# A three-stage attention and gated-layer kernel: partition maxima on TensorE, weight chunks two a unit, loads behind the first queries, shared score slots, a Prelu gate

## The chip, the cores and the metric

One program runs on one core of one Trainium2 chip. The metric is the device time of one execution in microseconds. The kernel before took 1237.77 us, the median of three runs (1237.25 to 1241.06). Matrix products are float32-accurate: every operand is held as a high and a low float16 half, and a product is three float16 matmuls.

## The reference

```
q_pool = q.reshape(B, H, S//2, 2, D).mean(axis=3)          # B 4, H 8, S 1152, D 64
scores = q_pool @ k^T / 8;  attn = exp(scores - max)
attn   = attn / (sum(attn) + 1e-9);  x = attn @ v           # x becomes 2304 x 512
h = x @ w_in                                                # 512 x 2048
g = h if h >= 1;  0 if h <= -1;  (h + 1)^2 / 4 between
y = g @ w_out                                               # 2048 x 512
out = max(y @ w1, y @ w2, y @ w3) @ w_out2                  # 512 x 768, 768 x 512
```

The weights arrive as 64-bit floats and are turned to float32 on the chip, chunk by chunk.

## The kernel before

The attention runs in 48 **units**, one for each batch, block of 192 pooled queries and pair of heads: 4 batches x 3 blocks x 4 pairs, so units 0 to 11 are the first batch. In a unit TensorE makes three score tiles of 128 x 1152 (`soft`, words `s0`, `s1`, `s2`); for each, VectorE takes the row maximum (L380), ScalarE turns it into a bias (L381) and takes the exponential with its row sum (L382). The exponentials are then turned (`turned`, words `t0`, `t1`, `t2`; `t-` is the third one of the unit before). In the first batch TensorE turns all three tiles in float32 (L418) and ScalarE copies them out (L429, L431); in later batches only the third goes this way, and two go through a float16 split and a transposing DMA. `shares` (word `r`) makes the reciprocals of the row sums, spreads them over 64 columns each (L396), lets TensorE turn them (L398, L399) and copies the result out (L401, L402). `av` (word `a1`) multiplies with the values of the unit before.

Score tiles and turned tiles come from one PSUM pool of two slots, handed out in the order of the code. The third turned tile's slot also holds the turned reciprocals.

Beside attention, word `d` takes one step of the two dense layers, from unit 5 on: `up_steps` makes two blocks of 128 rows of h for one block of tokens (L520) and gates them, `down_steps` makes one block of y (L545). The gate is one ScalarE pass (L525), three VectorE passes (L526 to L528), one ScalarE pass to float16 (L529) and one VectorE pass for the low half (L530).

Word `w` takes one step of preparing w_in and then w_out, in the first batch alone: load a chunk of 64-bit words, make float32 of it (`to_f32`: one ScalarE pass, L156, and four VectorE passes, L157 to L162), take its squares on ScalarE, and, with a scale per row, split it in halves (L148, L149). The table W_STEPS says how many `w` words of a unit act. The maxima over partitions that scale the whole weight are taken by GpSimd's partition_all_reduce (L214 for w_in, L244 for w_out). k and v of a batch come at the times in K0, V0 (first batch) and K1, V1: load, square, and split, where `split` puts the high half on GpSimd and the low half on VectorE (L259, L260).

What sets the order: TensorE's instructions stand in the order of the words (manual order). The other engines' streams and the issue order of the DMAs, all on SyncE's queue, come from the compiler's list scheduler, with priorities shifted by the code. Each engine runs its own stream in order. After the 48 units the rest of the dense steps run beside the loading of w1, w2, w3, and then the last stage, bound to TensorE.

Of the kernel before, what the change touches and what calls it, by code (L numbers as in the profile page):

```python
# [52 lines left out]
def body(ctx: ExitStack, tc: tile.TileContext, q, k, v, w_in, w_out, w1, w2, w3, w_o2, out):  # L53
    nc = tc.nc
# [207 lines left out]
    first = []  # L262

    def load(x, b, p, key):
        if b == 0 and key == "k" and p:

            if p == 1:
                first.append(ptp.tile([P, 2, 2 * KT, NB], F16, tag="pt", name="kn0"))
            w = 2 * KT * D
            n = first[0].rearrange("p a b c -> p (a b c)").bitcast(F32)[:, (p - 1) * w:p * w].rearrange(  # L270
                "p (a b c) -> p a b c", a=2, b=KT)
        else:
            n = nat.tile([P, 2, KT, D], F32, tag="nat", name=f"{key}n{b}_{p}")
# [596 lines left out]
```

## Time and profile before

| What | Value |
|---|---|
| median of three runs | 1237.77 us |
| the profiled execution | 1240.77 us |
| its span | 1239.0 us |
| TensorE busy | 1080.9 us (87%) |
| VectorE busy | 880.2 us (71%) |
| ScalarE busy | 744.0 us (60%) |
| GpSimd busy | 128.2 us (10%) |

The span runs from the first to the last instruction; the execution lasts 1.8 us longer. Busy shares are means over stages that differ: the first batch ends about 302 us into the span, the last unit about 867 us, and the last stage starts about 963 us.

### The profile page before, as it was taken

The numbers are of one execution on the slowest core, as the hardware profiler recorded it, in microseconds if no ns is written. First come the engines' busy times: TensorE is split into PE (matmuls) and PEld (weight loads), VectorE is DVE, ScalarE is ACT, GpSimd is POOL, SyncE is SP. The second block draws the span as 40 slices with busy tenths as digits, with TensorE's granted clock in tenths as the row PEclk, the third lists the DMA queues.
The fourth block names the chain that finished last, engine by engine and source line by source line (L and its number), as shares of the span: only waits on it lengthen the run. The fifth ranks groups of instructions, "written<-read, shape, count | busy, mean of one in ns | idle before, by whom it ended". The sixth has DMA issues, their size and how long they took to land. (4 is left out here: it accounts for less than half of the span.)

```text
span 1239.0 us, 26628 instructions
## 1 busy us (share of the span) xinstructions
PE 1080.9 (87%) x11058; PEld 885.8 (71%) x11058; DVE 880.2 (71%) x1550; ACT 744.0 (60%) x1337; POOL 128.2 (10%) x114
## 2 busy tenths in 40 slices
PE   2446577789999998999998999999887999999998
PEld 1234366577888887788887888888886776767774
DVE  4973586776999999989899999888798652322220
ACT  4865476776777787778788777778554411122111
POOL 1110000111100021210011300000221020100000
PEclk9668688799999998999999999999898999999999
DMA  7743135035865679865669866656544220000001
GB/s 227 229 133 94 69 98 153 14 81 143 165 110 110 122 138 185 176 127 112 114 116 190 169 110 102 110 99 121 182 131 133 75 67 17 10 27 18 17 18 43
DMA packets 273752, 134.89 MB, mean 109 GB/s; under 512 B 229088, under 2 KB 256736, under 8 KB 272608
## 3 DMA queue, kind: packets, MB, share of 16 engines
q1 hardware_dynamic: 273632, 133.20, 47.7%
q8 instruction: 86, 1.41, 0.5%
q14 instruction: 34, 0.28, 0.1%
HBM read 62.39 MB, written 9.44 MB: 58 GB/s over the span
## 5 line engine op out<-in xcount | busy, mean ns | idle before, releaser
L366 PE MATMUL sc<-kst,qst 128*64 128x512 f16 (+3 forms) x1152 | 176.2, 342 | 55.8 <-ACT pf L382 15.8
L769 PE MATMUL p<-yh,wm 128*128 128x288 f16 x1728 | 216.7, 287 | 6.5 <-POOL yh L740 5.4
L545 PE MATMUL py<-g,wou 128*128 128x192 f16 x2304 | 204.4, 250 | 14.9 <-ACT g L529 5.8
L545 PEld LDWEIGHTS <-wou 128*128 128x128 f16 x2304 | 194.1, 100 | 24.8 <-issue 21.8
L520 PE MATMUL ph<-xh,win 128*128 128x192 f16 x2304 | 204.8, 250 | 7.3 <-POOL xh L259 3.1
L380 DVE TENSOR_REDUCE st<-sc 128x1 f32<-128x1152 f32 x144 | 194.5, 1351 | 20.7 <-PE sc L366 20.3
L769 PEld LDWEIGHTS <-wm 128*128 128x128 f16 x1728 | 169.8, 98 | 53.0 <-issue 7.6
L520 PEld LDWEIGHTS <-win 128*128 128x128 f16 x2304 | 196.8, 100 | 10.2 <-issue 8.1
L382 ACT ACTIVATE pf<-sc,st,esc 128x1152 f32<-128x1152 f32 x144 | 188.7, 1310 | 4.2
L366 PEld LDWEIGHTS <-qst 128*64 128x64 f16 (+1 forms) x1152 | 85.2, 108 | 116.5 <-issue 54.0
L418 PE MATMUL tr<-ident,pf 128*128 128x128 f32 x648 | 97.8, 303 | 42.1 <-ACT pf L382 34.0
L418 PEld LDWEIGHTS tr<-ident,pf 128*128 128x128 f32 x648 | 82.3, 159 | 54.5 <-ACT pf L382 40.5
L436 DVE TENSOR_TENSOR hl<-pf,hl 128x1152 f16<-128x1152 f32 x72 | 98.3, 1366 | 4.8 <-ACT hl L435 2.1
L777 ACT ACTIVATE h<-mx 128x288 f16<-128x288 f32 x48 | 21.2, 442 | 132.1 <-DVE mx L775 132.1
L774 DVE TENSOR_TENSOR mx<-p,mx 128x288 f32<-128x288 f32 x48 | 21.9, 456 | 106.3 <-PE p L769 105.7
L454 PE MATMUL av<-pt,vhl 128*64 128x192 f16 x1944 | 87.6, 248 | 0.3 <-DMA pt<-hl 0.2
L454 PEld LDWEIGHTS <-vhl 128*64 128x64 f16 x1944 | 79.9, 110 | 9.9 <-issue 9.4
L435 ACT ACTIVATE hl<-pf 128x1152 f16<-128x1152 f32 x72 | 83.4, 1158 | 0.8
L529 ACT ACTIVATE g<-t,dgs 128x384 f16<-128x384 f32 x96 | 57.7, 608 | 40.5 <-DVE t L528 40.3
L381 ACT ACTIVATE st<-st,esc 128x1 f32<-128x1 f32 x144 | 41.4, 288 | 54.3 <-DVE st L380 54.1
L530 DVE SCALAR_TENSOR_TENSOR g<-t,dgs,g 128x384 f16<-128x384 f32 x96 | 62.8, 661 | 5.3 <-ACT g L529 5.2
L786 PE MATMUL po<-wo,h 128*128 128x512 f16 x288 | 64.3, 379 | 0.0
(169 smaller groups left out, 1323.4 us busy)
## 6 DMA issues: line engine op xcount, KB each, us to landing
kn<-in_k_dram SPq DMA_DIRECT2D x16, 576.0 KB, 4.3
vn<-in_v_dram SPq DMA_DIRECT2D x16, 576.0 KB, 4.3
raw_m<-in_moe_w_dram SPq DMA_DIRECT2D x12, 768.0 KB, 4.7
raw_in<-in_moe_w_in_dram SPq DMA_DIRECT2D x8, 1024.0 KB, 5.6
qn<-in_q_dram SPq DMA_DIRECT2D x24, 256.0 KB, 3.4
raw_ou<-in_moe_w_out_dram SPq DMA_DIRECT2D x10, 512.0 KB, 4.5
qst<-qst SPq DMA_DIRECT2D x48, 96.0 KB, 2.2
y_d<-ys SPq DMA_DIRECT2D x48, 96.0 KB, 2.0
```

Source lines behind the costliest of these rows:

```text
L366: nc.tensor.matmul(sc[m0:m1, n0:n1], qst[b, i, p][who][:, var, m0:m1], ks[:, h, n0:n1], start=(var == 0), stop=(var == 1))
L380: nc.vector.tensor_reduce(out=m, in_=sc, axis=AX.X, op=ALU.max, negate=True)
L382: nc.scalar.activation(out=pf, in_=sc, func=AF.Exp, bias=nb, scale=e, accum_out=sums[b, i, p][:, who:who + 1])
L418: nc.tensor.transpose(tr[:, c * P:(c + 1) * P], pf[:, c * P:(c + 1) * P], ident)
L435: nc.scalar.activation(out=hl[:, 0], in_=pf, func=AF.Copy)
L436: nc.vector.tensor_tensor(out=hl[:, 1], in0=pf, in1=hl[:, 0], op=ALU.subtract)
L454: nc.tensor.matmul(acc[64 * h:64 * h + 64], vhl[b, p][:, vi, h, c, :], pt[:, h, pi * KT + c, :], start=(c == 0 and e == 0), stop=(c == KT ...
L520: nc.tensor.matmul(ph[:, a], win[:, wi, kt, ff * P:(ff + 1) * P], x[:, xi, kt], start=(kt == 0 and e == 0), stop=(kt == KD - 1 and e == 2))
L530: nc.vector.scalar_tensor_tensor(out=g[:, 1, fs, :], in0=t2, scalar=gs, in1=g[:, 0, fs, :], op0=ALU.mult, op1=ALU.subtract)
L545: nc.tensor.matmul(py, wou[:, ff // 2, wi, ff % 2, m * P:(m + 1) * P], g[:, gi, ff, :], start=(ff == 0 and e == 0), stop=(ff == NF - 1 and ...
L769: nc.tensor.matmul(ph[:, :NB2], wm[:, wi, i, kt, ff * P:(ff + 1) * P], yh[:, yi, kt, n0:n0 + NB2], start=(kt == 0 and e == 0), stop=(kt == ...
L786: nc.tensor.matmul(po, h2t[b][:, hi, ff, t * P:(t + 1) * P], wo[:, wi, ff, :], start=(ff == 0 and e == 0), stop=(ff == NF2 - 1 and e == 2))
```

## The change

The list of edits:
- `all_max` is new: it turns a column, spread over 128, with TensorE, and VectorE takes the maximum along the free axis. It takes the place of both partition_all_reduce.
- In the first batch the words stand in another order (ORDER), and `t2` closes its own unit.
- W_AT names which `w` words of a unit act: two in units 0 to 3, four in unit 4, three in 5 to 7, two in 8; two more steps exist, since the maximum of w_in and the first loads of w_out are steps of their own. Three chunks of w_out are loaded ahead.
- k and v loads of the first batch have other times (K0, V0) and their own buffers; the second loads wait in the queue until the first queries' copies have been issued.
- The spreading copy of the reciprocals goes to GpSimd and covers two of the three columns.
- The gate is Prelu with slope 0.5 on ScalarE, then two VectorE passes instead of three; one factor 0.5 per batch falls away.

```diff
-K0 = ((-2, -2, -2), (-1, 0, 0), (0, 1, 1), (3, 5, 5))
+K0 = ((-2, -2, -2), (-1, 0, 1), (0, 2, 3), (3, 5, 6))
-W_STEPS = {0: 3, 1: 3, 2: 2, 3: 1, 4: 2, 5: 3, 6: 3, 7: 2, 8: 2}
+W_AT = {0: "13", 1: "13", 2: "13", 3: "13", 4: "0123", 5: "123", 6: "123", 7: "123", 8: "01"}
-ORDER = {True: "s0 t- d d r s1 t0 q s2 t1 a1 w d d w w",
-         False: "s0 t- d d r s1 t0 a1 s2 t1 q w d d w w"}
+ORDER = {True: "s0 w0 r d s1 d w1 t0 a1 q t1 w2 s2 d d w3 t2",
+         False: "s0 t- d d r s1 t0 a1 s2 t1 q d d"}
+    def all_max(dst, x, n, key):
+        ps = psg.tile([P, 512], F32, tag="g1", name=f"max_{key}")[:, :n * P].rearrange("p (a b) -> p a b", a=n)
+        for a in range(n):
+            nc.tensor.transpose(ps[:, a], x[:, a:a + 1].to_broadcast([P, P]), ident)
+        nc.vector.tensor_reduce(out=dst, in_=ps, axis=AX.X, op=ALU.max)
-        nc.gpsimd.partition_all_reduce(U_in, um[:, 0:2], P, RMAX)
+        yield
+        all_max(U_in, um, 2, "in")
-        nc.gpsimd.partition_all_reduce(U_ou, um[:, 1:2], P, RMAX)
+        all_max(U_ou, um[:, 1:2], 1, "ou")
+        for h in range(3):
+            fetch(h)
+        yield
-        rb = tp.tile([P, 3, 64], F32, tag="rb", bufs=2, name=f"rb{b}_{i}_{p}")
-        nc.vector.tensor_copy(out=rb, in_=sm.rearrange("p (a o) -> p a o", o=1).to_broadcast([P, 3, 64]))
+        rb = tp.tile([P, 2, 64], F32, tag="rb", bufs=2, name=f"rb{b}_{i}_{p}")
+        nc.gpsimd.tensor_copy(out=rb, in_=sm[:, 0:2].rearrange("p (a o) -> p a o", o=1).to_broadcast([P, 2, 64]))
-            nc.scalar.activation(out=t2, in_=ph, func=AF.Relu, scale=hh, bias=0.5)
-            nc.vector.tensor_scalar(out=rl, in0=t2, scalar1=1.0, scalar2=None, op0=ALU.min)
-            nc.vector.scalar_tensor_tensor(out=t2, in0=t2, scalar=2.0, in1=rl, op0=ALU.mult, op1=ALU.subtract)
-            nc.vector.tensor_tensor(out=t2, in0=t2, in1=rl, op=ALU.mult)
+            nc.scalar.activation(out=t2, in_=ph, func=AF.Prelu, scale=hh, bias=-1.0, alpha=0.5)
+            nc.vector.tensor_scalar(out=t2, in0=t2, scalar1=1.0, scalar2=0.0, op0=ALU.add, op1=ALU.max)
+            nc.vector.scalar_tensor_tensor(out=t2, in0=t2, scalar=1.0, in1=t2, op0=ALU.min, op1=ALU.mult)
-    first_k = issued["k"]
-    with tc.issue_after(first_k):
+    with tc.issue_after(issued["q"]):
```

What the code alone doesn't show is where the instructions then stand. On SyncE's queue, at the start of the program, before (kn, qn, vn are loads of k, q, v; raw_in is a chunk of w_in; kst and qst are turned k and q, and the two DMAs from qst to qst swap its halves):

```order
L297 DMA_TRANSPOSE kst_0_125<-kpre_0_124 128x18x128
L340 DMA_TRANSPOSE qst_0_0_149<-qpre_0_0_140 128x6x128
L274 DMA kn_159<-in_k_dram 128x2x576
L180 DMA raw_in_1_161<-in_moe_w_in_dram 128x2048
L342 DMA qst_0_0_149<-qst_0_0_149 64x768 x2
L304 DMA vn_0_178<-in_v_dram 128x2x576
```

And now:

```order
L302 DMA_TRANSPOSE kst_0_125<-kpre_0_124 128x18x128
L345 DMA_TRANSPOSE qst_0_0_149<-qpre_0_0_140 128x6x128
L347 DMA qst_0_0_149<-qst_0_0_149 64x768 x2
L279 DMA kn_1_159<-in_k_dram 128x2x576
L185 DMA raw_in_1_161<-in_moe_w_in_dram 128x2048
L309 DMA vn_0_178<-in_v_dram 128x2x576
```

The two swapping copies of the first queries moved ahead of a k load and of the second weight chunk.

On TensorE, in unit 2 (third pair of heads, first block), before (sc is a score tile, tr a turned tile, rb the spread reciprocals; of each score tile the first row stands):

```order
L366 MATMUL sc_0_2_1_526<-kst_2_214,qst_0_2_381 128x512
...
L418 MATMUL tr_0_2_0_547<-ident,pf_0_2_0_500 128x128 x9
...
L366 MATMUL sc_0_2_2_558<-kst_2_214,qst_0_2_381 64x512
...
L418 MATMUL tr_0_2_1_576<-ident,pf_0_2_1_534 128x128 x9
L449 MATMUL av_0_1_587<-pt_0_1_356,vn_1_313 64x192 x18
...
L366 MATMUL sc_0_3_0_630<-kst_3_404,qst_0_2_381 128x512
...
L418 MATMUL tr_0_2_2_645<-ident,pf_0_2_2_572 128x128 x9
```

And now:

```order
L371 MATMUL sc_0_2_1_504<-kst_2_259,qst_0_2_398 128x512
...
L423 MATMUL tr_0_2_0_528<-ident,pf_0_2_0_478 128x128 x9
L454 MATMUL av_0_1_539<-pt_0_1_350,vn_1_309 64x192 x18
L423 MATMUL tr_0_2_1_560<-ident,pf_0_2_1_512 128x128 x9
...
L371 MATMUL sc_0_2_2_571<-kst_2_259,qst_0_2_398 64x512
...
L423 MATMUL tr_0_2_2_612<-ident,pf_0_2_2_585 128x128 x9
...
L371 MATMUL sc_0_3_0_625<-kst_3_437,qst_0_2_398 128x512
...
L403 MATMUL tr_0_2_2_612<-ident,rb_0_2_641 128x128
```

Before, score tiles and turned tiles took turns, so every score tile got one slot and every turned tile the other. Now two score tiles follow each other, then two turned tiles, then one of each, and the slots change hands. The value product moved between the first two turned tiles, and the turned reciprocals stand right behind the next unit's first score tile.

On GpSimd, around the first partition maximum, before (qn and qpre are pooled queries and their halves, xh the halves of x, ISA an instruction around the custom one):

```order
L259 TENSOR_SCALAR qpre_1_2_1061<-qn_1_2_1057,sqq_1_2_1062 128x6x64
L335 TENSOR_TENSOR qn_2_0_1471<-qn_2_0_1471 128x6x64
L214 ISA
L214 ISA U_in<-um_in 128x2
L259 ISA
L259 TENSOR_SCALAR qpre_2_0_1475<-qn_2_0_1471,sqq_2_0_1476 128x6x64
L259 TENSOR_SCALAR xh_0_899<-xf_0_445,Uv_446 128x768
```

And now:

```order
L340 TENSOR_TENSOR qn_1_0_701<-qn_1_0_701 128x6x64
L274 TENSOR_SCALAR qpre_1_0_705<-qn_1_0_701,sqq_1_0_706 128x6x64
L401 COPY rb_0_1_498<-sm_0_1_299 128x128
L340 TENSOR_TENSOR qn_1_2_1081<-qn_1_2_1081 128x6x64
L274 TENSOR_SCALAR kpre_3_436<-kn_3_319,sb_121 128x18x64
L274 TENSOR_SCALAR qpre_1_2_1085<-qn_1_2_1081,sqq_1_2_1086 128x6x64
L401 COPY rb_0_2_641<-sm_0_2_477 128x128
```

The custom instruction with its two companions is gone from the stream, and copies of reciprocals stand between the query and key work.

## Rows read from the trace of the kernel before

**Rows 1.** Busy time by stretch: PE, PEld, DVE, ACT, POOL, granted clock, DMA share, GB/s.
```profile
24.53:115.54 91.01, 52.03 (x341) 35.86 (x342) 66.70 (x128) 64.08 (x101) 9.74 (x9) 0.74 0.52 147
115.54:150.22 34.68, 14.84 (x91) 10.12 (x90) 14.27 (x29) 13.40 (x22) 2.49 (x4) 0.61 0.29 98
150.22:302.00 151.78, 123.20 (x1124) 100.22 (x1123) 110.26 (x191) 108.03 (x183) 16.99 (x18) 0.91 0.36 101
302.00:432.00 130.00, 126.69 (x1573) 111.48 (x1573) 117.60 (x200) 101.64 (x191) 13.29 (x13) 0.99 0.66 124
432.00:552.00 120.00, 108.60 (x1307) 95.17 (x1303) 109.41 (x195) 91.24 (x170) 22.46 (x18) 0.96 0.80 158
642.00:732.00 90.00, 79.39 (x956) 69.55 (x953) 84.77 (x154) 68.33 (x127) 16.78 (x14) 0.96 0.84 161
732.00:867.00 135.00, 134.70 (x1714) 119.43 (x1713) 119.95 (x185) 107.69 (x201) 3.45 (x4) 1.00 0.59 106
867.00:963.00 96.00, 78.77 (x834) 72.65 (x833) 82.38 (x144) 52.16 (x85) 19.37 (x7) 0.89 0.48 150
963.00:1239.00 276.00, 270.90 (x2000) 192.23 (x1999) 84.88 (x184) 58.69 (x121) 11.69 (x12) 1.00 0.10 31
```

**Rows 2.** Timeline, GpSimd, unit 4: start, duration, instruction [idle before <- releaser].
```profile
117.89 0.99 POOL L335 TENSOR_TENSOR qn<-qn 128x384 f32<-128x384 f32 x1 [24.49 <-DMA qn<-in_q_dram]
126.97 0.37 POOL L214 PARTITION_ALL_REDUCE U_in<-um_in  x1 [8.09 <-issue]
134.33 0.58 POOL L259 TENSOR_SCALAR qpre<-qn,sqq 128x384 f16<-128x384 f32 x1 [6.99 <-issue]
```

**Rows 3.** Timeline, VectorE, the same stretch.
```profile
127.38 0.21 DVE L472 TENSOR_SCALAR Uv<-U_in,Uv 128x1 f32<-128x1 f32 x1 [7.27 <-POOL U_in L214]
...
134.94 0.62 DVE L260 SCALAR_TENSOR_TENSOR qpre<-qn,sqq,qpre 128x384 f16<-128x384 f32 x1 [6.85 <-POOL qpre L259]
```

**Rows 4.** Groups of instructions: busy us, mean ns of one | idle before.
```profile
L211 DVE TENSOR_REDUCE um_in<-sum_in 128x1 f32<-128x512 f32 x1 | 0.7, 692 | 0.2 <-PE sum_in L209 0.2
L396 DVE COPY rb<-sm 128x192 f32<-128x192 f32 x48 | 16.9, 352 | 1.4
L259 POOL TENSOR_SCALAR qpre<-qn,sqq 128x384 f16<-128x384 f32 x24 | 18.8, 783 | 143.9 <-ACT py L549 83.3 <-ACT st L381 20.6 <-ACT pt L424 12.4
L280 ACT ACT_TABLE_LOAD x1 | 1.3, 1283 | 0.7 <-PEq L857 0.7
```

**Rows 5.** Timeline, GpSimd, behind the second partition maximum.
```profile
235.93 0.90 POOL L259 TENSOR_SCALAR xh<-xf,Uv 128x768 f16<-128x768 f32 x1 [7.15 <-DVE st L380]
```

**Rows 6.** Timeline, TensorE, the first score tile.
```profile
16.09 1.14 PE L366 MATMUL sc<-kst,qst 128*128 128x512 f16 x3 [9.47 <-DMA qst<-qpre]
23.37 1.12 PE L366 MATMUL sc<-kst,qst 128*128 128x512 f16 x3 [6.14 <-DMA qst<-qst]
```

**Rows 7.** DMA issues: KB each, median us to landing.
```profile
qst<-qst SPq DMA_DIRECT2D x48, 96.0 KB, 2.2
```

**Rows 8.** Waits, 24.53 to 302 us: us in total, times, longest.
```profile
POOL qn L335 <- DMA qn<-in_q_dram: 114.1, 9, 29.4
DVE st L380 <- PE sc L366: 19.9, 14, 4.5
```

**Rows 9.** Gate multiplication L528 by stretch: DVE busy (count), clock, DMA share, GB/s.
```profile
150.22:302.00 151.78, 8.34 (x14) 0.91 0.36 101
432.00:552.00 120.00, 8.40 (x14) 0.96 0.80 158
642.00:732.00 90.00, 6.30 (x11) 0.96 0.84 161
867.00:963.00 96.00, 5.37 (x10) 0.89 0.48 150
```

**Rows 10.** Timeline, VectorE and GpSimd together, in unit 11.
```profile
285.92 1.38 POOL L335 TENSOR_TENSOR qn<-qn 128x384 f32<-128x384 f32 x1 [1.79 <-DVE rl L526]
...
286.48 1.23 DVE L528 TENSOR_TENSOR t<-t,rl 128x384 f32<-128x384 f32 x1
```

More of the change, by code (lines that the diff above doesn't have):

```diff
@@ L4 @@
 import concourse.tile as tile
-from concourse import bass_isa, mybir
+from concourse import mybir
 from concourse._compat import with_exitstack
@@ L16 @@
 DRAM = bass.MemoryType.DRAM
-RMAX = bass_isa.ReduceOp.max
-RADD = bass_isa.ReduceOp.add
 HO = (1, 0)
 POOL_FIRST = 10
-K0 = ((-2, -2, -2), (-1, 0, 0), (0, 1, 1), (3, 5, 5))
-V0 = ((0, 0, 0), (3, 4, 4), (6, 7, 7), (9, 10, 10))
+K0 = ((-2, -2, -2), (-1, 0, 1), (0, 2, 3), (3, 5, 6))
+V0 = ((0, 2, 3), (3, 5, 6), (5, 7, 8), (8, 10, 11))
 K1 = (-2, 0, 2)
 V1 = (1, 2, 3)
-W_STEPS = {0: 3, 1: 3, 2: 2, 3: 1, 4: 2, 5: 3, 6: 3, 7: 2, 8: 2}
+W_AT = {0: "13", 1: "13", 2: "13", 3: "13", 4: "0123", 5: "123", 6: "123", 7: "123", 8: "01"}
 OW = 130
 OD0, T0 = -150, 48
-ORDER = {True: "s0 t- d d r s1 t0 q s2 t1 a1 w d d w w",
-         False: "s0 t- d d r s1 t0 a1 s2 t1 q w d d w w"}
+ORDER = {True: "s0 w0 r d s1 d w1 t0 a1 q t1 w2 s2 d d w3 t2",
+         False: "s0 t- d d r s1 t0 a1 s2 t1 q d d"}
 DEPTH = 1
@@ L226, in w_ou_steps, with fetch @@
         sts.append(one[:, 4:6].rearrange("p a b -> p (a b)").bitcast(F32))
-        for h in range(NG):
+        raws = {}
+        def fetch(h):
             at_ = {0: 6, 1: 4, 3: 6}.get(h)
@@ L237, in w_ou_steps @@
                 load_q.dma_start(out=raw[:, f], in_=words(w_out[ff * P:(ff + 1) * P, :]))
-            to_f32(sts[h], raw.rearrange("p a b c -> p (a b) c"))
+            raws[h] = raw
+        for h in range(3):
+            fetch(h)
+        yield
+        for h in range(NG):
+            to_f32(sts[h], raws.pop(h).rearrange("p a b c -> p (a b) c"))
             nc.scalar.activation(out=wou[:, 0, 0].bitcast(BF16), in_=sts[h].rearrange("p (a b) -> p a b", a=2),
                                  func=AF.Square, accum_out=mx[:, h:h + 1])
+            for x in {0: (3,), 2: (4,), 4: (5,), 5: (6,), 6: (7,)}.get(h, ()):
+                fetch(x)
             yield
@@ L260, in split @@
         nc.vector.scalar_tensor_tensor(out=lo, in0=x, scalar=s, in1=hi, op0=ALU.mult, op1=ALU.subtract)
-    first = []
     def load(x, b, p, key):
[L265 to L273, printed above, removed]
+        n = nat.tile([P, 2, KT, D], F32, tag="nat", name=f"{key}n{b}_{p}")
         load_q.dma_start(out=n, in_=x[b, 2 * p:2 * p + 2].rearrange("h (p c) d -> p h c d", p=P))
@@ L393, in shares @@
         nc.vector.tensor_scalar(out=sm, in0=sm, scalar1=1e-9 * 2.0 ** 12, scalar2=None, op0=ALU.add)
-        rb = tp.tile([P, 3, 64], F32, tag="rb", bufs=2, name=f"rb{b}_{i}_{p}")
         nc.vector.reciprocal(out=sm, in_=sm)
-        nc.vector.tensor_copy(out=rb, in_=sm.rearrange("p (a o) -> p a o", o=1).to_broadcast([P, 3, 64]))
+        rb = tp.tile([P, 2, 64], F32, tag="rb", bufs=2, name=f"rb{b}_{i}_{p}")
+        nc.gpsimd.tensor_copy(out=rb, in_=sm[:, 0:2].rearrange("p (a o) -> p a o", o=1).to_broadcast([P, 2, 64]))
         r, half = R[b, i, p], slice(64, P)
-        nc.tensor.transpose(rs[:, 0:P], rb[:, 0:2].rearrange("p a o -> p (a o)"), ident)
-        nc.tensor.transpose(rs[:, P:2 * P], rb[:, 2, 0:1].to_broadcast([P, P]), ident)
+        nc.tensor.transpose(rs[:, 0:P], rb.rearrange("p a o -> p (a o)"), ident)
+        nc.tensor.transpose(rs[:, P:2 * P], sm[:, 2:3].to_broadcast([P, P]), ident)
         nc.scalar.activation(out=r, in_=rs[:, :NB], func=AF.Copy)
@@ L485, in scales @@
         hu = small.tile([P, 1], F32, tag="hu", name=f"hu{b}")
-        hh = small.tile([P, 1], F32, tag="hh", name=f"hh{b}")
         nc.vector.tensor_scalar(out=hu, in0=U_in[:, 1:2], scalar1=Uv[b][:, NPAIR:NPAIR + 1],
                                 scalar2=None, op0=ALU.mult)
-        nc.vector.tensor_scalar(out=hh, in0=Uv[b][:, NPAIR + 1:NPAIR + 2], scalar1=0.5, scalar2=None, op0=ALU.mult)
         gd = small.tile([P, 1], F32, tag="dgd", name=f"dgd{b}")
@@ L495, in scales @@
         nc.vector.reciprocal(out=gs, in_=gd)
-        dst[b] = hh, gd, gs
+        dst[b] = Uv[b][:, NPAIR + 1:NPAIR + 2], gd, gs
     room = dict(h=(psg, "g1"), y=(psg, "g1"), t2=tp, n=2)
@@ L608, in body @@
     behind, todo = {}, []
-    words_left = [3] * len(units)
     def attend(n, word):
@@ L637, in attend @@
         elif kind == "w":
-            words_left[n] -= 1
-            if words_left[n] < W_STEPS.get(n, 0):
+            if num in W_AT.get(n, ""):
                 with shift(OW):
```

1 line of the change is left out of this document (removed).

## The prediction

> **What bounds the kernel now.** I read the busy time by stretch first, cut where the stages change [rows 1]. Three kinds of stretch are to be seen. From 732 to 867 us TensorE is busy 134.7 of 135.0 us, and in the last stage, from 963 us, 270.9 of 276.0: there only TensorE's own work counts. From 302 to 432 us it is nearly so, 126.7 of 130.0. In the two stretches where the next batch's k and v are prepared (432 to 552, 642 to 732) TensorE lacks 11.4 and 10.6 us, and VectorE is busy 91% and 94%: VectorE bounds. The first batch, before 302 us, is bound by no engine: VectorE is busy 66.7 of 91.0 us in units 0 to 3, 14.3 of 34.7 in unit 4, 110.3 of 151.8 in units 5 to 11, and TensorE's granted clock is 0.74, 0.61 and 0.91. So the second thing to read is what the first batch waits for, from the timeline of unit 4 and the waits of the first batch.
>
> **Partition maxima by TensorE.** In unit 4 the custom reduction runs only 0.37 us, but GpSimd stands 8.09 us ahead of it and 6.99 us behind it for nothing that the trace shows [rows 2]. VectorE waits in both gaps, 7.27 us for the maximum and 6.85 us for the query half that GpSimd makes next [rows 3]: 14.1 us. In its place come two turns on TensorE and one VectorE maximum of 128 x 256; the nearest row, 128 x 512, takes 0.69 us [rows 4], so between nothing and 0.7, and with the two hops between engines I take 1.5 us for all. The gain is 12.6 us; at least 6 (only one gap goes, the other being covered by what else is late), at most 14.1. The second reduction, for w_out, leaves the same kind of gap, 7.15 us, in front of the half of x that TensorE needs [rows 5]. Most of it lies beside other work; I take 3, bounds 0 and 7.2.
>
> **Loads behind the first queries.** The first score tile's second half starts at 23.37 us, having waited 6.14 us for the swapped halves [rows 6]; such a copy lands in 2.2 us [rows 7], but behind it in the queue stood a k load and a 1 MB chunk. With the copies ahead, the tile can be ready some 4 us earlier. The k load and the chunk come later in exchange, and so does what they feed. I take 2 us gained; bounds 4 gained, 3 lost.
>
> **Two slots for scores and turns, weight steps spread.** A score tile no longer waits for the exponential of the tile ahead of it, only for the tile two places back. VectorE waited 19.9 us in 14 pieces for scores between 24.5 and 302 us [rows 8]; that is what the sharing can shorten, and it leaves VectorE free to take the weight steps, which were three a unit early and are now two. For units 0 to 3 VectorE's 66.7 us at the 94% that it reaches in 642 to 732 [rows 1] would need 71 us instead of 91: at most 20 gained, at least nothing, since the same conversions stand in one stream with the maxima. I take VectorE at 80%, 83 us: 8 gained. For units 5 to 11 VectorE loses 8.3 us of gate products [rows 9] and seven copies of 0.352 [rows 4], which leaves 99.5 us; TensorE's 123.2 us bound the stretch instead, 127 us at the 97% of the stretch behind it. So at most 25 gained, at least 0. I take 10 beyond the 3 above, nearer to zero, because scores, maximum, exponential and turn still follow each other within a unit. The turned reciprocals now stand right behind the next first score tile; if their copy is late, TensorE waits there with the second score tile behind it. TensorE's clock should rise with its share in these units; I count nothing for it.
>
> **Prelu gate and the GpSimd copy.** The product L528 goes, 96 times. Prelu takes the place of a Relu of the same size from the same slot, and the two passes left have the forms of L526 and L527, so I price them as before; the trace has no Prelu, and a slower one by 0.1 us would lie on ScalarE, which is idle a quarter of the time. VectorE gets back 8.40 and 6.30 us of products in the two k and v stretches [rows 9], and with half as many copies, 12 or 13 of 0.352 us [rows 4], 4.4 us more: 19.1 us, where TensorE lacks 22.0 in all. I take two thirds, 13 us, since some of the lack is waiting on loads and on ScalarE; bounds 0 and 22. From 302 to 432 TensorE has 3.3 us to give; I take 1. Between 867 and 963 ten gates give back 5.4 us [rows 9] of VectorE's 82.4 in 96 us [rows 1]; loads and weight work fill the rest, so 2, bounds 0 and 5.4. From 732 to 867 and from 963 on, nothing.
>
> The copy costs GpSimd a third of the 0.783 us that 128 x 384 takes [rows 4], 0.26 us, or all of it at most. What hides it is the turn of the third tile and the next score tile ahead of the reciprocals.
>
> The trace shows GpSimd and VectorE hindering each other: the gate product that started 0.56 us after a query sum on GpSimd took 1.23 us [rows 10], twice what the others take (8.40 us for 14). The Trainium skill, page "SBUF — State Buffer", section "Who interferes with whom", says why: the two share one port pair, which one of them holds for a whole instruction. By that rule each of the 48 copies can hold up a VectorE pass by its own 0.26 us, and the copy moved gives back 0.09 us instead of 0.352; in the k and v stretches that is 3 us less, and the sum below would be 49 instead of 52. I leave the sum as it is, since a copy need not meet such a pass.
>
> **The sum.** First batch 12.6 + 3 + 2 + 8 + 10 = 35.6; then 1 + 13 + 2: together 51.6 us. The profiled execution took 1240.77 us (its span 1239.0 and 1.8 around it), so 1189.2 by its own time; the median of the three runs lies 3.0 us lower, which would be 1186. I predict 1188 us.
>
> **The rivals.**
> - *Only the stalls go.* The conversions, the maxima and the exponentials of the first batch stand in line as before, and sharing slots only moves the wait. For it: in units 0 to 3 the same chunks pass through the same VectorE stream, and the loads come in at 147 GB/s all the while [rows 1]. Against it: VectorE's waits for scores. Gains 12.6 + 3 + 2 + 10 + 2 = 30: 1211 us. Chance 0.17.
> - *The first batch fills up.* Units 0 to 3 take 71 us and units 5 to 11 take 127; with 19 in the k and v stretches and 4 in the tail the gain is 12.6 + 2 + 20 + 25 + 1 + 19 + 4 = 84: 1157 us. For it: VectorE does reach 91 to 94% elsewhere. Chance 0.10.
> - *Slower: the copy on GpSimd becomes the wait.* GpSimd works in order, and it stands 114.1 us in nine waits for query loads, 12.7 each [rows 8]. A copy of reciprocals queued behind such a wait holds TensorE at the turned reciprocals, and the second score tile with it. In the new stream the copies of units 0 to 3 do stand behind query work. Four full holds, 51 us, use up the sum; from there it decides. With five, 63 us, the time is 1240.8 - 51.6 + 63 = 1252. Against it: those waits began when GpSimd had nothing else to do, so little of them falls after the sums are known. Chance 0.05.
> - *Prelu needs another table than the exponential.* Then ScalarE would load tables twice a gate at 1.283 us [rows 4], 96 times: 246 us on an engine that has half that free, so well over 1300 us. Against it: the new program holds one table load, as the old one did. Chance 0.01.
> - *Nothing to measure*, gains and holds cancel: 1240 us, chance 0.03.
>
> On the fourth, the Trainium skill, page "ScalarE: Activation LUTs", section "Table sets: the hidden batching unit", gives about 2.7 us for each change of set and names the cheap functions in every set without naming Prelu. By that figure the price would be some 500 us; no run shown here has a Prelu.
>
> **How the numbers follow.** The forecast has 0.64; its own range is 1172 to 1205 us (terms at half and at one and a half of the uncertain 36 us, rounded). The range for 8 in 10 takes in the first rival with its spread and most of the way to the second: 1160 to 1222. Left out are the lower half of the second rival, the slower cases and the unchanged one. A difference under 0.3%, about 3.7 us, can't be told from none. Faster: 0.64 + 0.17 + 0.10 = 0.91; same 0.03; slower 0.05 + 0.01 = 0.06.
>
> **What would show it.** Right: no gaps of 7 to 8 us on GpSimd around unit 4, and unit 4 at some 20 us instead of 34.7; the first score tile's second half before 20 us; the first batch's end near 266 us instead of 302; TensorE's lack in the k and v stretches at 9 instead of 22 us; 96 VectorE passes fewer, and 48 copies on GpSimd of about 0.26 us. Wrong: if the first batch ends later than 285 us (then the first rival), if TensorE waits long for a GpSimd copy at the turned reciprocals (the third), or if table loads stand between the gates (the fourth). What would make the forecast wrong without any of these is a weight load or the w_out halves coming late in the new order, with TensorE waiting at the first block of y.

## The result, and the profile after

The changed kernel takes 1203.7 us (median of four runs, 1202.4 to 1207.5) where the kernel before took 1239.4 beside it: a ratio of 0.971, interval 0.967 to 0.975. The forecast was 1188 with an own range of 1172 to 1205. The direction is right and the time lies inside both ranges, in its own range by 1.3 us; the gain is 36 us instead of 51.6, and the time is nearer to the first rival's 1211 than to 1188. The profiled span is 1201.7 us against 1239.0.

The busy time by stretch, cut near the same places of the program as [rows 1]; columns: stretch, length, then busy us (and instructions) of PE, PEld, DVE, ACT, POOL, granted clock, DMA share, GB/s.
```profile
20.10:109.34 89.24, 53.88 (x336) 37.95 (x338) 68.45 (x128) 67.65 (x104) 10.06 (x13) 0.77 0.66 198
109.34:131.48 22.14, 14.68 (x107) 9.91 (x102) 17.76 (x35) 13.59 (x21) 3.79 (x4) 0.80 0.31 103
131.48:274.11 142.63, 119.61 (x1117) 98.75 (x1118) 92.51 (x163) 106.94 (x182) 20.10 (x24) 0.91 0.34 93
404.00:523.00 119.00, 108.22 (x1351) 94.82 (x1347) 104.80 (x176) 91.17 (x172) 23.07 (x25) 0.99 0.82 162
612.00:700.00 88.00, 80.10 (x982) 70.69 (x981) 78.91 (x139) 68.88 (x129) 17.58 (x18) 0.98 0.83 167
700.00:832.00 132.00, 131.47 (x1674) 116.30 (x1672) 105.69 (x151) 104.08 (x197) 5.93 (x14) 1.00 0.60 109
```
The first batch ends at 274 us; 266 was expected. Unit 4 (second row) lost 12.5 us. Units 0 to 3 (first row) hardly moved, and VectorE is as busy there as before. In units 5 to 11 VectorE lost 17 us of work and the stretch 8 ([rows 1] ends that stretch 0.9 us later, at 302 us). In the two k and v stretches TensorE still lacks 10.8 and 7.9 us.

Unit 4, timeline of GpSimd, TensorE and VectorE (start, duration, instruction, idle before and its releaser). The rows answer to [rows 2, 3].
```profile
111.25 0.99 POOL L340 TENSOR_TENSOR qn<-qn 128x384 f32<-128x384 f32 x1 [4.96 <-DMA qn<-in_q_dram]
113.63 0.59 POOL L274 TENSOR_SCALAR qpre<-qn,sqq 128x384 f16<-128x384 f32 x1 [1.39 <-DVE sqq L96]
115.53 0.46 PE L108 MATMUL max_in<-ident,um_in 128*128 128x128 f32 x2
117.00 0.41 DVE L109 TENSOR_REDUCE U_in<-max_in 128x2 f32<-128x256 f32 x1
```
From the turn's start (115.53) to the maximum's end (117.41) it takes 1.9 us, of which 0.87 are work; the trace shows no engine waiting for it, and GpSimd's gaps of 8.09 and 6.99 us, which nothing in the trace explained, are gone.

The first score tile's second half, TensorE's timeline; it answers to [rows 6], 23.37 us there.
```profile
18.92 2.53 PE L371 MATMUL sc<-kst,qst 128*128 128x512 f16 x7 [1.60 <-DMA qst<-qst]
```
The priced operations, from the groups of instructions (busy us, mean ns of one, idle before); they answer to [rows 4, 9].
```profile
L527 ACT ACTIVATE t<-ph,Uv 128x384 f32<-128x384 f32 x96 | 54.8, 574 | 7.6 <-PE ph L523 4.2 <-DVE g L531 2.8 <-PE av L459 0.5
L528 DVE TENSOR_SCALAR t<-t 128x384 f32<-128x384 f32 x96 | 39.4, 413 | 27.4 <-ACT t L527 27.2
L529 DVE SCALAR_TENSOR_TENSOR t<-t 128x384 f32<-128x384 f32 x96 | 56.8, 594 | 1.4
L401 POOL COPY rb<-sm 128x128 f32<-128x128 f32 x48 | 14.9, 310 | 323.6 <-DVE sm L399 295.1 <-ACT ys L549 18.4 <-DVE ub L95 8.4
L285 ACT ACT_TABLE_LOAD x1 | 1.3, 1283 | 0.7 <-PEq L855 0.7
```
Prelu costs 574 ns, what Relu cost, with one table load in the whole program. The two VectorE passes cost what L526 and L527 did (421 and 596 ns), and the copy on GpSimd 0.31 us.

Where the time went, by the start of each unit's first maximum on VectorE, in us (u0 is that of unit 0; "rest" runs from unit 47 to the end). Each row is one profiled execution, so a difference of a few us in one column may be chance; the rows below the second are the experiments. Units 28 to 31 took 58.0 to 58.8 us and units 40 to 46 took 101.5 to 102.0 in all of them.

| kernel | u0 | 0-3 | 4 | 5-8 | 9-11 | 12-19 | 20-27 | 32-39 | rest |
|---|---|---|---|---|---|---|---|---|---|
| before | 24.5 | 91.0 | 34.7 | 83.6 | 67.3 | 122.9 | 135.7 | 132.8 | 386.1 |
| after | 20.1 | 89.2 | 22.1 | 86.4 | 56.2 | 122.6 | 131.6 | 129.1 | 384.7 |
| only_maxima | 24.1 | 93.8 | 19.2 | 92.9 | 65.4 | 123.3 | 135.7 | 133.1 | 387.5 |
| in_max_only | 24.3 | 94.1 | 19.7 | 79.4 | 90.3 | 121.7 | 135.4 | 135.0 | 386.3 |
| maxima_fetch | 24.8 | 93.4 | 19.2 | 78.8 | 66.5 | 123.3 | 136.0 | 135.1 | 385.8 |
| old_steps | 20.2 | 89.5 | 18.4 | 77.7 | 68.4 | 121.6 | 132.6 | 131.2 | 382.0 |
| late_turn | 20.2 | 89.6 | 20.3 | 91.9 | 62.2 | 124.4 | 131.4 | 131.6 | 380.8 |
| no_conv | 20.3 | 89.3 | 22.6 | 85.6 | 56.5 | 121.9 | 131.2 | 131.6 | 381.4 |
| no_loads | 20.1 | 91.2 | 21.6 | 84.4 | 56.2 | 123.1 | 132.3 | 129.9 | 381.7 |
| q_early | 20.5 | 85.1 | 23.7 | 84.0 | 56.1 | 121.0 | 132.6 | 131.7 | 384.4 |
| old_gate | 20.4 | 88.8 | 24.4 | 86.4 | 55.9 | 123.3 | 134.8 | 135.2 | 388.3 |
| r_vector | 20.0 | 86.3 | 23.2 | 88.2 | 56.6 | 122.9 | 134.8 | 134.5 | 380.0 |
| k_early | 20.1 | 88.7 | 25.0 | 82.3 | 54.1 | 122.9 | 136.4 | 128.6 | 382.0 |
| both_early | 20.0 | 84.4 | 25.3 | 86.0 | 54.6 | 120.4 | 131.9 | 128.7 | 384.7 |

### The profile page after: what moved, and what is told of

It is laid out like the page before. It is cut to its first block, busy times and chain, and to the rows that moved or that the text cites. A ratio compares the mean times of both kernels' runs of the same rounds, so it can differ in the third digit from the quotient of the medians.

```text
span 1201.7 us, 26667 instructions
## 1 busy us (share of the span) xinstructions
PE 1074.7 (89%) x11061; PEld 883.2 (73%) x11061; DVE 822.1 (68%) x1404; ACT 739.6 (62%) x1337; POOL 139.1 (12%) x160
## 4 chain that ended last, share of the span: by engine, by line
PE 44%; DVE 4%; ACT 3%; issue 3%; DMA 3%; POOL 0%; ACTq 0%; SPq 0%; POOLq 0%; DVEq 0%
PE p L767 18%; PE py L546 7%; PE po L784 5%; PE ph L523 5%; PE sc L371 4%; PE av L459 3%; PE tr L423 1%; DMA pt<-hl 1%; DVE st L385 1%; ACT pf L387 1%; PE por L798 1%; ACT hl L440 1%; DVE st_m L167 1%; DVE hl L441 0%; DMA raw_m<-in_moe_w_dram 0%
## 5 line engine op out<-in xcount | busy, mean ns | idle before, releaser
L784 PE MATMUL po<-wo,h 128*128 128x512 f16 x288 | 64.3, 379 | 0.0
L430 DVE TENSOR_TENSOR pt<-tr,pt 128x1152 f16<-128x1152 f32 x36 | 48.8, 1356 | 18.8 <-ACT pt L429 18.8
```

The source lines that it names most:

```text
L784: nc.tensor.matmul(po, h2t[b][:, hi, ff, t * P:(t + 1) * P], wo[:, wi, ff, :], start=(ff == 0 and e == 0), stop=(ff == NF2 - 1 and e == 2))
```

## The experiments

**The maxima.** First the kernel before with both maxima by TensorE, and nothing else.
```diff
-        nc.gpsimd.partition_all_reduce(U_in, um[:, 0:2], P, RMAX)
+        all_max(U_in, um, 2, "in")
-        nc.gpsimd.partition_all_reduce(U_ou, um[:, 1:2], P, RMAX)
+        all_max(U_ou, um[:, 1:2], 1, "ou")
```
only_maxima: 

> The kernel before with one thing changed: both partition maxima by two (one) transposes and a VectorE maximum. Theory A (the stalls around the custom reduction were the end of unit 4, and nothing late stands behind them): unit 4 falls from 34.7 to about 22 us, the w_out maximum gives 1 to 3, so 1223 to 1227 us against 1239. Rival B (something else of unit 4, a query load or the weight steps, is late anyway and fills half of it): unit 4 stays above 27 us and the time above 1231.

Measured: 1237.1 us against 1241.3, ratio 0.997 (0.996 to 0.998). Unit 4 fell by 15.5 us, more than A said, and units 5 to 8 took 9.3 back, units 0 to 3 another 2.8. So neither: the gain is there and is lost elsewhere. Timeline of all engines, unit 7:
```profile
197.33 1.00 SPq L244 DMA_DIRECT2D raw_ou<-in_moe_w_out_dram  x2
202.62 1.12 ACT L163 ACTIVATE raw_ou<-raw_ou 128x1024 f32<-128x1024 f32 x1 [3.48 <-DMA raw_ou<-in_moe_w_out_dram]
210.05 0.15 DVE L97 TENSOR_SCALAR um_ou<-um_ou 128x1 f32<-128x1 f32 x1
210.26 0.47 PE L110 MATMUL max_ou<-ident,um_ou 128*128 128x128 f32 x1 [15.43 <-DVE um_ou L97]
```
The last w_out piece is issued at 197.33, behind query loads. Its conversion, squares and maximum end at 210, and TensorE, which works in the order written for it, has stood at the w_out maximum for 15.43 us.

Next the first maximum alone.
```diff
-        nc.gpsimd.partition_all_reduce(U_in, um[:, 0:2], P, RMAX)
+        all_max(U_in, um, 2, "in")
```

in_max_only: 

> The kernel before with the first partition maximum alone by TensorE; the one for w_out stays on GpSimd. When both were changed alone, unit 4 gave 15.5 us, but TensorE then stood 15.4 us at the turn of the w_out maximum, which waits in TensorE's written order for a VectorE value that comes late. Theory A (that wait took the gain): without it the time is 1226 to 1230 us against 1241. Rival B (units 5 to 8 are bound by the weight chunks that come in and are converted, whatever unit 4 does): 1235 to 1239.

Measured: 1249.1 us, ratio 1.006 (1.004 to 1.008): slower than before, a miss for both. Timeline of the engines behind that maximum:
```profile
223.48 0.38 POOL L251 PARTITION_ALL_REDUCE U_ou<-um_ou  x1 [5.66 <-issue]
231.41 0.58 POOL L266 TENSOR_SCALAR qpre<-qn,sqq 128x384 f16<-128x384 f32 x1 [7.56 <-issue]
232.03 0.62 DVE L267 SCALAR_TENSOR_TENSOR qpre<-qn,sqq,qpre 128x384 f16<-128x384 f32 x1 [7.86 <-POOL qpre L266]
233.87 1.15 ACT L155 ACTIVATE wou<-wou,s_ou 128x1024 f16<-128x1024 f32 x1 [8.17 <-DVE wou L156]
236.01 2.18 PE L425 MATMUL tr<-ident,pf 128*128 128x128 f32 x9 [10.86 <-ACT R L409]
```
Here GpSimd's gap of 7.56 us holds a query half, VectorE waits for it, ScalarE for VectorE, and TensorE 10.86 us for ScalarE. In the kernel before that same gap, 7.15 us [rows 5], lay mostly beside other work. Units 9 to 11 grew by 23 us: besides this wait, TensorE waits there 6.2 us for the halves of w_out at the first blocks of y (1.6 in the kernel before), and its own busy time is 64.3 us at a granted clock of 0.83 instead of 56.4 at 0.97.

Then both maxima with one more piece of the change: the loads of w_out taken out of the conversion steps.
```diff
...
-        for h in range(NG):
+        raws = {}
+        def fetch(h):
...
-            to_f32(sts[h], raw.rearrange("p a b c -> p (a b) c"))
+            raws[h] = raw
+        for h in range(3):
+            fetch(h)
+        for h in range(NG):
+            to_f32(sts[h], raws.pop(h).rearrange("p a b c -> p (a b) c"))
...
+            for x in {0: (3,), 2: (4,), 4: (5,), 5: (6,), 6: (7,)}.get(h, ()):
+                fetch(x)
```
maxima_fetch: 

> The kernel before with both partition maxima by TensorE and, from the change, the loads of the w_out pieces taken out of the conversion steps: three pieces at once, each later one right behind the conversion that frees its place. Theory A (with the maxima changed alone, TensorE stood 15.4 us at the w_out maximum because the last w_out piece was issued late, behind query loads): that wait falls under 4 us and the time is 1222 to 1228 us against 1241. Rival B (the conversions of the pieces are late, not their loads): the wait stays above 10 us and the time is 1234 to 1240.

Measured: 1224.6 us, ratio 0.987 (0.986 to 0.989), as A said: 12 us more than without the loads. The last piece is issued at 164.51 instead of 197.33, TensorE's turn for the maximum stands at 196.16 without a wait, and units 5 to 8 take 78.8 us instead of 92.9 (SyncE's queue and TensorE):
```profile
164.51 0.84 SPq L245 DMA_DIRECT2D raw_ou<-in_moe_w_out_dram  x2
196.16 0.32 PE L110 MATMUL max_ou<-ident,um_ou 128*128 128x128 f32 x1
```
The maxima alone do not have this gain. The loads alone were not run, so how much of it they would bring without the maxima stays open.

**The order of the first batch.** The changed kernel with the word order and the step places of before.
```diff
-ORDER = {True: "s0 w0 r d s1 d w1 t0 a1 q t1 w2 s2 d d w3 t2",
+ORDER = {True: "s0 t- d d r s1 t0 q s2 t1 a1 w0 d d w1 w2",
-W_AT = {0: "13", 1: "13", 2: "13", 3: "13", 4: "0123", 5: "123", 6: "123", 7: "123", 8: "01"}
+W_AT = {0: "012", 1: "012", 2: "12", 3: "2", 4: "12", 5: "012", 6: "012", 7: "12", 8: "12"}
...
-        yield
         all_max(U_in, um, 2, "in")
...
-        yield
```
old_steps: 

> The changed kernel with the word order of before in the first batch (the third tile's turn behind the next unit's first score tile, weight steps at the end of a unit, three in units 0 and 1); the loads, the maxima, the gate and the copy stay changed. Theory A, as predicted (the new order gave units 0 to 3 and 5 to 11 together 10 to 18 us): 1213 to 1221 us. Rival B (the new order gave nothing in the first nine units, since the third turn, now in its own unit, waits 3 to 5 us for its exponential each time): 1200 to 1208.

Measured: 1200.9 us, ratio 0.967 (0.964 to 0.969); B, and if anything below the changed kernel (the intervals overlap). The new order moved time from units 9 to 11 into units 4 to 8, 164.5 us with the old order and 164.7 with the new from unit 4 to 11.

Then only the third turn moved back.
```diff
-ORDER = {True: "s0 w0 r d s1 d w1 t0 a1 q t1 w2 s2 d d w3 t2",
+ORDER = {True: "s0 w0 t- r d s1 d w1 t0 a1 q t1 w2 s2 d d w3",
```
late_turn: 

> The changed kernel with one word moved: the third tile's turn stands behind the next unit's first score tile, as in before, and all else keeps its new place. Theory B (TensorE's waits for the third exponential, 22 us in units 0 to 3 and 26 in units 4 to 8, are the price of the word's new place): a score tile of 1.2 to 2.1 us fills each, twelve times, and the first batch ends 10 to 20 us sooner, 1184 to 1194 us. Rival C (the third exponential ends late because ScalarE and VectorE have the weight conversions in line, so the wait only moves to the next turn): 1200 to 1208.

Measured: 1214.1 us, ratio 0.977 (0.974 to 0.980): slower than the changed kernel, a miss for both, C the nearer. Between units 4 and 11 TensorE's waits for exponentials fell from 27.1 to 17.9 us, but its waits for copies of turned tiles grew from 0.6 to 15.7, and those for GpSimd's copies of the reciprocals from 0.6 to 3.5 (in units 0 to 3 from none to 5.2). With six tiles in turn on two slots, a word moved also changes whom each later tile waits for.

**What sets units 0 to 3.** VectorE's conversions lightened, in one kernel, and six of the eight w_in chunks not loaded, in another.
```diff
-    def to_f32(dst, raw):
+    def to_f32(dst, raw, short=False):
...
         nc.vector.tensor_scalar(out=dst, in0=dst, scalar1=F64_MIN, scalar2=F64_MAX, op0=ALU.max, op1=ALU.min)
+        if short:
+            return
...
-                to_f32(st[:, c], raw)
+                to_f32(st[:, c], raw, True)
```
no_conv: 

> The changed kernel without three of the four VectorE passes that turn each of the eight w_in chunks into single precision (the weights are wrong then; the loads, the ScalarE passes and all later work stay): VectorE has 25 us less to do in units 0 to 3. Theory A (the conversions in VectorE's line set the pace of units 0 to 3): units 0 to 3 take under 76 us instead of 89, 1182 to 1192 in all. Rival B (the loads, and the chain from score tile to maximum, exponential and turn, set it): over 83 us, 1196 to 1204 in all.

```diff
-            if n < 2 * KD:
+            if 2 <= n < 2 * KD:
+                raws.append(kept[n % 2])
+            elif n < 2:
...
+                kept.append(raw)
```
no_loads: 

> The changed kernel with only the first two of the eight w_in chunks loaded; the other six conversions take the same two chunks again (the weights are wrong then, all engine work stays): 6.3 MB less in units 0 to 3. Theory A (loads set the pace of units 0 to 3, since taking 25 us of conversions from VectorE left them at 89.3 us): they take under 80 us, 1185 to 1194 in all. Rival B (the chain within a unit on the in-order engines sets it, whatever the loads): 85 us or more, 1198 to 1206 in all.

Measured: 1203.7 and 1204.7 us, ratios 0.970 (0.967 to 0.973) and 0.972 (0.970 to 0.973). Units 0 to 3, the row by stretch of each:
```profile
20.30:109.60 89.30, 52.00 (x336) 36.63 (x338) 49.16 (x107) 67.39 (x104) 10.99 (x13) 0.85 0.65 199
```
```profile
20.10:111.30 91.20, 53.48 (x336) 36.36 (x338) 63.93 (x124) 65.66 (x101) 13.51 (x13) 0.77 0.47 125
```
VectorE busy 49 instead of 68 us in the first, 125 instead of 198 GB/s in the second, and the same 89 to 91 us: B of both. What is left by exclusion is the chain within a unit, through ScalarE's line; no run took both conversions and loads away, and none lightened ScalarE's own share of the conversions. The changed kernel's rows show one link, ScalarE and TensorE in unit 1:
```profile
59.63 0.29 ACT L386 ACTIVATE st<-st,esc 128x1 f32<-128x1 f32 x1
63.52 0.52 ACT L341 ACTIVATE qpre<-qn 128x384 bf16<-128x384 f32 x1 [3.60 <-POOL qn L340]
64.04 1.29 ACT L387 ACTIVATE pf<-sc,st,esc 128x1152 f32<-128x1152 f32 x1
65.48 2.18 PE L423 MATMUL tr<-ident,pf 128*128 128x128 f32 x9 [8.86 <-ACT pf L387]
```
The exponential's scores, maximum and bias are there at 59.92, but the query square in front of it waits for its load (through GpSimd's sum of the query).

So the query pair was prepared one unit earlier.
```diff
-            if n % 2 == 1 and n + 1 < len(units):
-                q_prep(*units[n + 1])
+            if n % 2 == 0 and n + 2 < len(units):
+                q_prep(*units[n + 2])
```
q_early: 

> The changed kernel with each pair's query load and preparation one unit earlier. Theory A (in units 0 to 3 ScalarE's line is stopped by the query square, which waits for its load, with the third exponential and so TensorE's turn behind it, 8.9 us in the longest case): the turns wait under 12 us for exponentials in units 0 to 3 instead of 22, which take 79 to 84 us instead of 89, and the time is 1190 to 1198 us. Rival B (the queue is full; a query load that goes ahead makes a weight chunk or a k load late): units 0 to 3 take 87 to 91 us, the time is 1200 to 1206.

Measured: 1200.5 us, ratio 0.968 (0.966 to 0.969); units 0 to 3 at 85.1. The 8.86 became 5.42:
```profile
61.19 2.18 PE L423 MATMUL tr<-ident,pf 128*128 128x128 f32 x9 [5.42 <-ACT pf L387]
```
Yet in units 0 to 3 the turns wait for exponentials as long as before, 23.2 us instead of 22.1 (A: under 12); what went is a score tile's wait of 4.8 for one, and waits for copies of the reciprocals came up (6.4 us instead of 5.8 for the turned ones, 2.5 instead of none for GpSimd's). The length of units 0 to 3 lies between the theories, the time is B's, and the difference to the changed kernel is inside the intervals.

**The k and v stretches.** The old gate in the changed kernel:
```diff
...
-            nc.scalar.activation(out=t2, in_=ph, func=AF.Prelu, scale=hh, bias=-1.0, alpha=0.5)
-            nc.vector.tensor_scalar(out=t2, in0=t2, scalar1=1.0, scalar2=0.0, op0=ALU.add, op1=ALU.max)
-            nc.vector.scalar_tensor_tensor(out=t2, in0=t2, scalar=1.0, in1=t2, op0=ALU.min, op1=ALU.mult)
+            nc.scalar.activation(out=t2, in_=ph, func=AF.Relu, scale=hh, bias=0.5)
+            nc.vector.tensor_scalar(out=rl, in0=t2, scalar1=1.0, scalar2=None, op0=ALU.min)
+            nc.vector.scalar_tensor_tensor(out=t2, in0=t2, scalar=2.0, in1=rl, op0=ALU.mult, op1=ALU.subtract)
+            nc.vector.tensor_tensor(out=t2, in0=t2, in1=rl, op=ALU.mult)
```
old_gate: 

> The changed kernel with the gate of before (Relu and three VectorE products instead of Prelu and two). Theory A, as predicted (VectorE bounds the two stretches where k and v of the next batch are prepared, units 20 to 28 and 32 to 40): each of them grows by 5 to 6 us and the tail by 2, so 1216 to 1222 us. Rival B (TensorE waits there for ScalarE's copies of the turned reciprocals, which stand in ScalarE's line behind a square that waits for a k load, so VectorE's share hardly counts): each grows by under 2 us, the whole 1204 to 1210.

The copies of the turned reciprocals on VectorE:
```diff
-        nc.scalar.activation(out=r, in_=rs[:, :NB], func=AF.Copy)
-        nc.scalar.activation(out=r[half, P:NB], in_=rs[half, NB:2 * P], func=AF.Copy)
+        nc.vector.tensor_copy(out=r, in_=rs[:, :NB])
+        nc.vector.tensor_copy(out=r[half, P:NB], in_=rs[half, NB:2 * P])
```
r_vector: 

> The changed kernel with the two copies of the turned reciprocals out of PSUM on VectorE instead of ScalarE. Theory A (VectorE bounds the k and v stretches): 96 more passes there cost time, 1206 to 1212 us. Rival B (the second score tile waits for those copies in ScalarE's line): the waits of a score tile for the copy, 5.2 and 4.5 us in the two stretches, go nearly to nothing, and the time is 1194 to 1200.

The k loads ahead:
```diff
-K1 = (-2, 0, 2)
+K1 = (-4, 0, 2)
...
-    nat = at.enter_context(tc.tile_pool(name="nat", bufs=2, side="right"))
+    nat = at.enter_context(tc.tile_pool(name="nat", bufs=3, side="right"))
```
k_early: 

> The changed kernel with three buffers instead of two for natural k and v, and each k load of a later batch issued two thirds of a unit earlier; no engine has less to do. Theory A (VectorE bounds the k and v stretches): within 2 us of the changed kernel, 1202 to 1206. Rival B (ScalarE's square of k, waiting 5.8 and 5.0 us for the load, holds up the copies that a score tile waits for): ScalarE's waits for k loads fall under 1.5 us a stretch, each stretch gets 2 to 4 us shorter, and the time is 1195 to 1200.

The wait that B speaks of, in the changed kernel's timeline (SyncE's queue, ScalarE, TensorE):
```profile
466.42 0.54 SPq L279 DMA_DIRECT2D kn<-in_k_dram  x1
471.22 1.16 ACT L285 ACTIVATE kpre<-kn 128x1152 bf16<-128x1152 f32 x1 [2.68 <-DMA kn<-in_k_dram]
473.90 0.32 ACT L406 ACTIVATE R<-tr 128x192 f32<-128x192 f32 x1
474.74 0.22 ACT L407 ACTIVATE R<-tr 64x64 f32<-64x64 f32 x1
475.01 1.17 PE L371 MATMUL sc<-kst,qst 128*64 128x512 f16 x12 [2.23 <-ACT R L407]
```
Measured: old_gate 1214.2 us (the profiled execution, 1219.5, is the slowest of its four), ratio 0.977 (0.975 to 0.979); r_vector 1207.2, 0.973 (0.970 to 0.975); k_early 1199.4, 0.965 (0.963 to 0.968). What TensorE lacks (stretch minus its busy time) and its main waits, in us:

| kernel | 20-27: lacks | of it R | xf | exp | 32-39: lacks | of it R | xf | exp |
|---|---|---|---|---|---|---|---|---|
| before | 11.5 | 4.7 | 3.1 | 3.0 | 11.1 | 5.0 | 2.4 | 3.1 |
| after | 10.8 | 5.2 | 2.3 | 1.6 | 8.5 | 4.5 | 1.8 | 1.9 |
| old_gate | 11.1 | 3.4 | 3.8 | 3.3 | 11.2 | 3.9 | 3.7 | 2.9 |
| r_vector | 12.0 | 1.4 | 7.5 | 1.9 | 11.8 | 1.4 | 7.1 | 2.2 |
| k_early | 12.1 | 0 | 1.7 | 5.9 | 6.6 | 0 | 1.6 | 4.9 |

(R: the copies of the turned reciprocals; xf: the scaled attention output on VectorE; exp: the exponential.) With the copies on VectorE the wait for them falls to 1.4 us, as B said, and the time does not fall, as A said: the scaled output, which is made from them in VectorE's line, is late instead. With the k loads ahead the wait for the copies is gone entirely, and what is late next is the exponential, in units 20 to 27 also one turn by DMA; why that one was late the rows don't settle. TensorE there, k_early:
```profile
442.83 2.18 PE L423 MATMUL tr<-ident,pf 128*128 128x128 f32 x9 [3.82 <-ACT pf L387]
504.02 4.53 PE L459 MATMUL av<-pt,vhl 128*64 128x192 f16 x54 [4.45 <-DMA pt<-hl]
```
So k_early met B's time without B's reason: units 20 to 27 got 4.8 us longer and units 32 to 39 only 0.5 shorter; in the profiled execution, 1.6 us under the changed kernel's, units 5 to 11 got 6.2 shorter. The gate's price is between the theories: 3.2 and 6.1 us in the two stretches, 7 us in all by the ratios and 10 by the medians.

**Both early.** The edits of q_early and k_early together.
```diff
-            if n % 2 == 1 and n + 1 < len(units):
+            if n % 2 == 0 and n + 2 < len(units):
...
-K1 = (-2, 0, 2)
+K1 = (-4, 0, 2)
...
```

both_early: 

> The changed kernel with each query pair prepared one unit earlier, and with three buffers for natural k and v and k loads of later batches two thirds of a unit earlier. Alone the two gave 3 and 4 to 7 us. Theory A (they take away waits of ScalarE's line in different stretches: the query square in units 0 to 3, the k square in units 20 to 28 and 32 to 40): 1192 to 1197 us. Rival B (one queue issues all loads and turns by DMA, and what goes ahead in it makes another transfer late): 1198 to 1204 us.

Measured: 1196.6 us, ratio 0.962 (0.959 to 0.966), the time that A said, and below the changed kernel's interval. A's reason holds for one of the two places: units 0 to 3 take 84.4 us instead of 89.2, but units 20 to 27 and 32 to 39 stay at 131.9 and 128.7 (131.6 and 129.1 in the changed kernel). It has the lowest median here; its interval overlaps that of k_early.

## Why the prediction was partly right

By the traces 37.3 us of span are gone. The runs assign some 27 to 30 of them: about 16 to the maxima with the w_out loads (maxima_fetch), 7 to 10 to the gate (old_gate), and 4.4 at the start, which every kernel with the new queue order has, if the three add up. The rest was not traced to one edit. Step by step:

- *Maximum in unit 4*, 12.6 predicted, 12.5 measured. The place and the cause are right; that the size fits so well is in part luck. Alone the maxima gave 15.5 in unit 4, and with the old word order in the changed kernel 16.3, so the new order, with four weight steps in unit 4, took some 3 to 4 back. The step had also taken the gain as unit 4's own: alone it is 0.3% in all, and it needs the w_out loads.
- *Maximum for w_out*, "3, bounds 0 and 7.2": mis-sized, since it is not a sum of its own. On GpSimd it cost TensorE 3.1 us in the kernel before (its wait for that half of x) and 10.9 in in_max_only; on TensorE it cost 15.4 with the old loads and no wait with the new ones. The prediction priced the moved instruction and not what TensorE's written order does when its operand is late; it had named late w_out halves only as a thing that could make it wrong.
- *Loads behind the first queries*, 2 predicted, 4.4 measured at the first maximum. Its upper bound, 4, was the better value: the loss set against the gain, later k and weight loads, was not seen there.
- *Units 0 to 3*, 8 predicted, 1.8 measured. This step failed. It took VectorE's share as the limit; taking 19 us of VectorE's work away there changed nothing, nor did taking the loads away. By exclusion, and by TensorE's waits for exponentials (27 us in the changed kernel, 24 and 30 in those two), the chain through ScalarE's line is the likeliest limit. Two runs shortened a link of it: q_early gained 4 us there, and r_vector, which takes the copies of the turned reciprocals out of ScalarE's line and gives VectorE more to do, 2.9. It is not shown beyond that: in old_steps the waits for exponentials are only 7 us, other waits take their place, and the stretch is 89.5 us all the same.
- *Units 5 to 11*, 10 and 3 predicted, 8.2 measured. The size is near, the reason is not: sharing slots and spreading steps gives nothing measurable (old_steps). What pays from unit 4 to 11 are the maxima with the w_out loads (maxima_fetch: 164.5 us from 185.6).
- *k and v stretches*, 13 predicted, 7.8 measured over units 20 to 27 and 32 to 39. VectorE lost 18 us of busy time there, as counted. TensorE's lack fell by 0.8 and 2.6 only; the rest is TensorE's own busy time, 124.2 to 120.8 and 121.7 to 120.6, at a granted clock of 0.99 instead of 0.96 and 0.97. "VectorE bounds" was read from a busy share of 91 to 94%. Taking work off VectorE there does pay (old_gate), but less than its share, since the waits move on to ScalarE's copies, the scaled output or the exponential. The sum priced TensorE's lack alone, which was to fall from 22.0 to 9 us and is 18.7 by the rows above; that TensorE's own time would fall as well was not in it, and makes up for a part.
- *302 to 432 and tail*, 1 and 2 predicted, 0.3 and 1.4 measured; with runs of one kernel 5 us apart that is no finding.

Of the rivals, "only the stalls go" (1211) had the better picture of units 0 to 3, and, if the 10 in its sum stands for the k and v stretches, it was nearer there too; it missed on units 4 to 11 (15.6 us against 20.8). The forecast's own range holds by 1.3 us, with units 0 to 3 at a quarter of their term and units 5 to 11 and the k and v stretches at about six tenths. GpSimd's copy did not become the wait: TensorE waited 0.6 us for it between units 4 and 11, and in late_turn, the worst case here, 8.7 us in the first batch. The copy was not tried alone, so its worth stays open. The Trainium skill, page "SBUF — State Buffer", section "Who interferes with whom", says that VectorE and GpSimd keep each other out of a shared port. The trace agrees at one of the 48 copies, and there it is GpSimd that is held. 47 copies take 0.29 to 0.30 us; the one that starts 0.24 us into a VectorE pass with two inputs takes 1.10, and TensorE's wait of 0.6 us follows it:
```profile
130.37 1.20 DVE L165 SCALAR_TENSOR_TENSOR wou<-raw_ou,wou 128x1024 uint32<-128x1024 uint32 x1
130.61 1.10 POOL L401 COPY rb<-sm 128x128 f32<-128x128 f32 x1 [7.12 <-DVE sm L399]
131.77 0.47 PE L403 MATMUL tr<-ident,rb 128*128 128x128 f32 x1 [0.63 <-POOL rb L401]
```
For VectorE the copies show no price: the gate passes take 413, 594 and 653 ns where they took 421, 596 and 661. The fourth rival fell with the single table load. Its "half that free" does not come out of the rows either, since ScalarE is idle 495 us of the span before (1239.0 less 744.0), twice the 246; nothing hung on it. On Prelu's price the Trainium skill, page "ScalarE activation tables: per-element evaluation and per-set limits", section "What a function is on this engine", says that with the same operands the instruction costs the same whichever table is read; the trace agrees, 574 ns for the Relu before and 574 for the Prelu.

## What to carry to other kernels

An engine's busy share, even 94%, doesn't say how much removing its work shortens the stretch: read which wait ends last, and what stands ahead of its releaser in that engine's own line. A reduction moved onto an in-order engine brings its operand's lateness with it, so move the load that feeds it in the same edit. One edit can be worth 4 us alone and 16 together with a second, and half of it can cost 8, so a sum of terms needs a check of which terms presuppose each other.
